# V in full-height blocks with half-zero copies, and a table and three splits moved to other places in VectorE's order

## The chip, the cores and the metric

The kernel runs on one core of one Trainium2 chip. The metric is device time in microseconds (us) of one launch. A core has a matmul engine (TensorE, PE), VectorE (DVE), ScalarE (ACT), GpSimd (POOL) and SyncE (SP), which work in parallel, each in the order of its own instructions, and wait for each other by semaphores. SBUF is the memory of 128 partitions that engines work on, PSUM the one that PE writes to. Transfers (DMAs) are issued from the queue of an engine, here mostly SP's; those that gather or scatter rows by index are built by GpSimd.

## The reference, cut to what matters

Three stages in a row: attention with a window, a gated dense layer, and a layer of eight experts in which a token goes to one expert or to none.

```python
# attention: 2 batches x 8 heads x 768 tokens x 64
scores = q @ k.T / 8 + bias(distance)       # only 8 global keys and the last 96 keys are kept
a = softmax(scores); attn = a @ v           # then heads side by side: x is 1536 x 512
# gated dense layer
xn = x / rms(x) * rms_g
x = (silu(xn @ w_gate) * (xn @ w_val)) @ w_out          # 512 -> 1536 -> 512
# experts
do_compute = x @ w_skip > 0
e = argmax(x @ w_gate2);  g = softmax(x @ w_gate2)[e]
out = x;  out[do] = x + g * (relu(x @ w1[e]) @ w2[e])   # 8 experts, 512 -> 1024 -> 512
```

## The kernel before, in words

**Attention.** Heads are taken in eight pairs, one head in each half of the partitions. A pair has three items, each of two blocks of 128 queries. Item by item PE makes scores (`qk`), DVE adds the bias and takes row maxima (`ttr`, L259), ACT takes exponentials (`exp`, L270), GpSimd or DVE scales (`norm`), PE transposes (`trans`) and multiplies with V (`pv`, L332). These steps run one loop turn apart: in turn t the loop makes the scores of item t and the product with V of item t − 3. A query block sees three blocks of keys, and of these one with half of its rows only. For such a half, V stands a second time in SBUF, the other half of the partitions cleared: tile `vlo` holds the rows of the even blocks on partitions 0 to 63, `vhi` those of the odd ones on 64 to 127. There are three pairs of such tiles, cleared once at the start by memsets on DVE and GpSimd, and reused by pair number modulo 3. `loadv` (L224) issues on SP the transfer of V itself (`vp`, 128 partitions) and of the two half tiles. Loads of a pair are issued two pairs ahead, in the order of a list on SP. The weights of the dense layer (`wraw`) come on the same queue, from the fourth pair of V on.

**Dense layer.** Products are made at full precision from parts: a weight is split in a high part (ACT casts) and a low part (DVE subtracts). The second product goes tile by tile, 12 tiles of 128 tokens. Into its order of matmuls the routing of each tile is hung by hooks: at given positions of the last tile, `routed(10)`, `tenth` (the ranks, selection and gates of tile 10) and `adds` are called. After the last tile comes the last routing: its logits, ranks, and the first rows of expert 0, one chain through PE, ACT and DVE. PE fills its waits there with products that nobody reads (`keep`).

**Experts.** Eight experts and one additional block of 64 tokens (`Job`, for an expert that has more than 128; it comes eighth in the row of nine, at index 7) run the same steps: `gather` (GpSimd fetches token rows by index), `tx` (transposition, high part `exh`, low part `exl`), `up` (first product), `relu`, `th` (transposition of the result into `ehh` and `ehl`), `down` (second product, into PSUM `epy`), `put` (gate, addition, scatter). A weight of 128 x 1024 comes as `eraw` and is split by ACT (`ewh`, L870) and DVE (`ewl`, L879). The order of these is fixed by the program: `split_next(n)` splits the next n chunks, in the row of all experts, `load_next(n)` issues the next n loads into free buffers. Buffers are a list of slots: those of the dense layer's output weights join it by `free_wo`. After expert 0's first product `jobs` makes a table of which expert needs additional blocks and how many (15 short DVE operations on counts that a small product gives), and `job_select` picks the block of the first. After the ninth `put` the number of blocks is read from the table as the bound of a loop, which here runs no further turn.

Of the kernel before, what the change touches and what calls it, by code (L numbers as in the profile page):

```python
# [127 lines left out]
def general_attention(s):  # L128

    nc, tc = s.nc, s.tc  # L130
    with tc.tile_pool(name="ga", bufs=1) as p, tc.tile_pool(name="gap", bufs=1, space=PSUM) as ps:
# [3 lines left out]
        with tc.For_i(0, 8, 1) as pr:  # L135
            slope = p.tile([128, 2], F32, name="gslope")
            nc.vector.tensor_copy(slope, slopes[:, ds(pr, 1), :].rearrange("p a b -> p (a b)"))
            for hh in range(2):
# [7 lines left out]
                v = p.tile([128, 11, 64], F32, name="gv")  # L146
                nc.sync.dma_start(v.rearrange("p (a b) d -> p a (b d)", a=1),
                                  s.vx.rearrange("a p n -> p a n")[:, ds(pr, 1), 704 * hh:704 * hh + 704])
                xo = p.tile([64, 768], F32, name="gxo")
# [52 lines left out]
def attention(s, rms):  # L202
# [21 lines left out]
    def loadv(pr):  # L224
        v = vs[pr] = ap.tile([128, 2, 11, 64], F32, name="vp", bufs=3)
        nc.sync.dma_start(v.rearrange("p h b d -> p (h b d)"), s.vx[pr, :, 0:1408])
        lo, hi = halves[pr % 3]
        nc.sync.dma_start(lo[0:64].rearrange("p h b d -> p (h b d)"), s.vx[pr, 0:64, 1408:2176])
        nc.sync.dma_start(hi[64:128].rearrange("p h b d -> p (h b d)"), s.vx[pr, 64:128, 1408:2048])

# [79 lines left out]
    def pv(it, r):  # L310
        pr, g = it
        pts = [(outs[it, z // 4][1], z % 4) for z in range(3 * r, 3 * r + 3)]

        if r == 0:
            po = s.bank([128, 512], "po")
            outs[it] = po[:, 0:256].rearrange("p (a b) -> p a b", a=2)
            s.spare = po[:, 256:512]
        po = outs[it]
        i = 2 * g + r
        lo, hi = halves[pr % 3]  # L320

        def terms(hh):
            a, b = slice(64 * hh, 64 * hh + 64), slice(64 - 64 * hh, 128 - 64 * hh)
            yield 0, 1, lo[:, hh, i], a
            if i:
                yield 0, 0, vs[pr][:, hh, 2 * i - 1], a
                yield 1, 1, hi[:, hh, i - 1], b
            yield 1, 2, vs[pr][:, hh, 2 * i], b

        for n, two in enumerate(zip(terms(0), terms(1))):  # L330
            for hh, (x, k, v, c) in enumerate(two):
                nc.tensor.matmul(po[64 * hh:64 * hh + 64, r, 64 * x:64 * x + 64], lhsT=v,  # L332
                                 rhs=pts[k][0][:, pts[k][1], c], start=i == 0 or n % 2 == 0, stop=i == 0 or n % 2 == 1)

    def out(it):
# [5 lines left out]
    n = len(items)  # L341
    halves = [(ap.tile([128, 2, 6, 64], F32, name=f"vlo{z}", bufs=1),
               ap.tile([128, 2, 5, 64], F32, name=f"vhi{z}", bufs=1)) for z in range(3)]
    es += [ap.tile([128, 2, 384], F32, name=f"es{z}", bufs=1) for z in range(3)]
    load(0)
    nc.gpsimd.memset(es[0][:, 0, 192:256], 0.0)
    for lo, hi in halves:
        nc.vector.memset(lo[64:128], 0.0)
        nc.gpsimd.memset(hi[0:64], 0.0)
    yield  # L350
# [392 lines left out]
def run(*parts):  # L743

    parts = list(parts)
    while parts:
        parts = [p for p in parts if next(p, FAR) is None]
# [13 lines left out]

def jobs(s, pool):

    nc, V = s.nc, s.nc.vector
    ps = s.ps_m.tile([128, 8], F32, name="cnt", tag="misc", bufs=1)
    nc.tensor.matmul(ps, lhsT=s.ones16, rhs=s.cum[:, 12, :], start=True, stop=True)
    s.i64 = pool.tile([128, 8, 22], F32, name="i64", bufs=1)
# [3 lines left out]
    nc.gpsimd.iota(s.i23, pattern=[[1, 23], [0, 8]], base=0, channel_multiplier=0,  # L771
                   allow_small_or_imprecise_dtypes=True)
    cnt = pool.tile([128, 8, 1], F32, name="cnts", bufs=1)
    V.tensor_copy(cnt.rearrange("p e a -> p (e a)"), ps)
# [70 lines left out]
class Expert:  # L845
# [37 lines left out]
    def split(self, c, hi, lo):  # L883
        self.high(c, hi)
        self.low(c, lo)
# [80 lines left out]
class Job(Expert):  # L966
# [54 lines left out]
    def down(self):  # L1021
        s = self.s
        self.y = s.ps_e.tile([128, 512], F32, name="epy", bufs=1)
        for k in range(8):
            self.products(self.y, self.hc[:, k], slice(512 * (k % 2), 512 * (k % 2) + 512),
                          *self.w[4 + k // 2][:2], k == 0, k == 7)
        for k in range(4, 8):
            self.done(k)
# [14 lines left out]
def attn_moe_kernel(ctx, tc, qx, kx, vx, rel, ints, wgv, w_out, rms_g, w9, w9t, w1, w2, out):  # L1043
# [317 lines left out]
    def tenth():  # L1361
        ranks(s, 10)
        choose(10, s.rk[10], s.oh[:, 10, 0:1])
        run(select(s, 10), gates(s, 10))

    def adds():
        add(s.x2[9], first[9], start=True)
        add(s.early, s.ident)
        free_wo(0, 3)

    def keep(n):
# [6 lines left out]
        (0, 2): lambda: turn(s, 10), (0, 5): early, (0, 9): lambda: routed(10),  # L1378
        (256, 4): lambda: turn(s, 11, 0), (256, 6): tenth, (256, 10): adds})
    idle = s.ps_m.tile([128, 512], F32, name="idle", tag="misc", bufs=1)  # L1380
    logits(s, 11, range(2))
# [29 lines left out]
    s.slots.add(s.epool, ["raw8"])  # L1411
    s.ps_e = pool(phase3, "ps_e", space=PSUM)
    experts[0].tx(x0)
    exps(s, 11)
    ranks(s, 11, s.ps_m, "misc")
    run(select(s, 11))

    def gathers():
        p = ids(s.ps_m, "misc", False)
        for t in range(9, 12):  # L1420
            nc.tensor.matmul(p, lhsT=s.sel[t][:, 0:128], rhs=s.val[:, t, 0, :], start=False, stop=t == 11)
        gi, si = indices(s, s.ixpool, p, 8, "s")
        for x in experts:
            if x is not job:
                x.gi, x.si = gi[:, x.e:x.e + 1], si[:, x.e:x.e + 1]
        for e in (1, 0, 2, 3):
            experts[e].gather()

        load_next(8, nc.gpsimd)

    experts[0].up(gathers)
    run(gates(s, 11))
    experts[0].relu()
    for t in range(9, 12):
# [15 lines left out]

    def split(n):
        split_next(n)
        load_next(max(0, len(s.slots.free) - 5))

    split(4)
    for j in range(9):
        if j:
            experts[j].th()
            split(1)
        if 1 <= j and j + 3 < 9:  # L1460
# [7 lines left out]
        if j == 0:  # L1468
            jobs(s, s.epool)
            job.gi, job.si, job.gate = job_select(s, s.epool, tabs[0:64, 1], slice(0, 1))  # L1470
        experts[j].down()
        split(3)
        experts[j].put()
    more = nc.values_load(s.eji[0:1, 23:24], min_val=1, max_val=22,  # L1474
                          skip_runtime_bounds_check_because="at most 22 blocks beyond the first ones")
    s.slots.free.sort(key=lambda x: x[1])
# [19 lines left out]
def layout(q, k, v):  # L1496
# [11 lines left out]
    for i in range(1, 6):  # L1508
        rows.append(np.concatenate([np.arange(128 * i - 96, 128 * i), np.arange(32)]))
        rows.append(np.arange(128 * i, 128 * i + 128))  # L1510
    vx = v[:, :, np.stack(rows, axis=1), :].reshape(B * H // 2, 2, 128, 11, D).transpose(0, 2, 1, 3, 4)
    half = np.zeros((B * H // 2, 128, 2, 6, D), v.dtype)
    half[:, 0:64] = vx[:, 0:64, :, 0::2]
    half[:, 64:128].reshape(B * H // 2, 64, 12 * D)[:, :, 0:10 * D] = \
        vx[:, 64:128, :, 1::2].reshape(B * H // 2, 64, 10 * D)
    return qx, kT[:, :, cols], np.concatenate([x.reshape(B * H // 2, 128, -1) for x in (vx, half)], axis=2)

# [50 lines left out]
```

## Time and profile before

| | |
|---|---|
| time, median of 3 runs | 533.31 us (532.67 to 535.36) |
| profiled execution | 531.11 us, span 529.4 us, mean clock of TensorE 0.995 |
| PE busy | 507.3 us, 96% of the span |
| DVE, ACT, GpSimd busy | 400.4, 265.5, 147.5 us |
| moved by DMA | 86.44 MB |

Attention runs to about 86 us, the dense layer and the routing of its tiles to about 397, the last routing to about 407, the experts to 522, and the last output and the end of the launch to 529.4. In a row of a timeline stand the start in us from the span's beginning, the duration, engine, line, operation, output <- inputs with their partitions x elements, the number of instructions that the row groups, and in brackets how long the engine was idle just before and what ended that. An idle engine costs time only if what waits for it reaches the end.

### The profile page before, as it was taken

The page shows a single profiled execution, that of the slowest core. Times are in us where ns is not written, and L with a number is a line of the kernel's source. Part 1 is how long each engine was busy: PE and PEld are TensorE (multiplying, and loading weights), DVE is VectorE, ACT ScalarE, POOL GpSimd, SP SyncE. Part 2 cuts the span into 40 slices and gives each one's busy share as a digit, 9 for nine tenths or more (in the row PEclk, how much of TensorE's full clock was granted, in tenths as well). Part 3 has the DMA queues.
Part 4 walks back from the last instruction along what each step waited for, and adds up shares of the span by engine and source line. Part 5 has one row for each costly group of instructions (what it writes and reads, how often), then busy time and mean ns, then how long its engine had stood idle before and what let it go on. Part 6 is the DMA issues. An engine that isn't in the chain of part 4 may idle for free. (4 is left out here: it accounts for less than half of the span.)

```text
span 529.4 us, 9730 instructions
## 1 busy us (share of the span) xinstructions
PE 507.3 (96%) x3389; PEld 413.6 (78%) x3389; DVE 400.4 (76%) x988; ACT 265.5 (50%) x618; POOL 147.5 (28%) x201
## 2 busy tenths in 40 slices
PE   7798999999999999999999999999999999999994
PEld 6676778888888888778888887877898778888763
DVE  7789896588887788588854467767743699999981
ACT  3898993333232332323323525425521779888860
POOL 4666772112222222212211000000000703666101
PEclk9999999999999999999999999999999999999997
DMA  5997811322332323323217213313771899999300
GB/s 183 303 310 228 271 34 43 139 80 85 116 111 82 125 87 113 119 80 119 81 42 252 86 41 119 120 40 127 239 279 41 307 399 396 399 400 384 120 16 16
DMA packets 31391, 86.44 MB, mean 163 GB/s; under 512 B 3875, under 2 KB 4271, under 8 KB 31336
## 3 DMA queue, kind: packets, MB, share of 16 engines
q1 hardware_dynamic: 26856, 74.52, 41.0%
q0 software_dynamic: 2608, 8.09, 4.0%
q10 hardware_dynamic: 1872, 3.15, 1.7%
q8 instruction: 28, 0.46, 0.4%
q14 instruction: 27, 0.22, 0.1%
HBM read 78.05 MB, written 8.53 MB: 164 GB/s over the span
## 5 line engine op out<-in xcount | busy, mean ns | idle before, releaser
L547 PE MATMUL ps<-xh,wh 128*128 128x512 f32 x272 | 106.3, 391 | 1.4 <-DVE h L567 1.4
L547 PE MATMUL ps<-xl,wh 128*128 128x512 f32 x272 | 106.1, 390 | 0.0
L547 PE MATMUL ps<-xh,wl 128*128 128x512 f32 x272 | 106.0, 390 | 0.0
L879 DVE TENSOR_TENSOR ewl<-eraw,ewh 128x1024 fp32r<-128x1024 f32 x72 | 83.4, 1215 | 7.7 <-ACT ewh L870 7.6
L870 ACT CAST ewh<-eraw 128x1024 fp32r<-128x1024 f32 x72 | 71.3, 1054 | 7.0 <-DVE ewl L879 6.8
L498 DVE SCALAR_TENSOR_TENSOR wraw<-f64t,wraw 128x512 f32<-128x512 f32 x36 | 43.7, 1214 | 29.6 <-ACT f64t L496 29.6
L625 PE MATMUL px<-woh,hh 128*128 128x512 f32 (+1 forms) x156 | 61.3, 393 | 0.0
L547 PEld LDWEIGHTS ps<-xh,wh 128*128 128x128 f32 x272 | 51.1, 188 | 12.2 <-DVE h L567 1.8
L547 PEld LDWEIGHTS ps<-xh,wl 128*128 128x128 f32 x272 | 51.1, 188 | 10.4
L547 PEld LDWEIGHTS ps<-xl,wh 128*128 128x128 f32 x272 | 51.1, 188 | 10.3
L625 PE MATMUL px<-woh,hl 128*128 128x512 f32 (+1 forms) x156 | 58.5, 375 | 0.0
L625 PE MATMUL px<-wol,hh 128*128 128x512 f32 (+1 forms) x156 | 58.3, 374 | 0.0
L511 POOL TENSOR_TENSOR wl<-f64t,wh 128x512 fp32r<-128x512 f32 x23 | 29.7, 1293 | 98.4 <-ACT wh L510 60.7
L510 ACT CAST wh<-f64t 128x512 fp32r<-128x512 f32 x24 | 14.9, 622 | 79.8 <-DVE f64t L508 79.8
L270 ACT ACTIVATE es<-es,m 128x192 f32<-128x192 f32 (+1 forms) x96 | 41.2, 432 | 6.4 <-DVE m L259 6.4
L287 POOL TENSOR_SCALAR es<-es,z 128x192 f32<-128x192 f32 (+1 forms) x94 | 36.9, 412 | 24.7 <-DVE z L279 10.7
L579 DVE TENSOR_TENSOR hl<-h,hh 128x256 fp32r<-128x256 f32 x72 | 25.4, 422 | 17.9 <-ACT hh L578 17.8
L625 PEld LDWEIGHTS px<-woh,hl 128*128 128x128 f32 x156 | 29.3, 188 | 5.6
L625 PEld LDWEIGHTS px<-woh,hh 128*128 128x128 f32 x156 | 29.4, 188 | 5.5 <-issue 0.8
L625 PEld LDWEIGHTS px<-wol,hh 128*128 128x128 f32 x156 | 29.4, 189 | 4.2
L1357 POOL DMA_INDIRECT early<-xm,si_f x1 | 1.3, 1301 | 106.8 <-DMA out_dram<-x 106.8
L259 DVE CUSTOM_DVE_ANT_0 es<-sc,bias 128x192 f32<-128x192 f32 (+1 forms) x96 | 27.0, 337 | 5.4 <-PE sc L248 3.6
(240 smaller groups left out, 1035.4 us busy)
## 6 DMA issues: line engine op xcount, KB each, us to landing
eraw<-in_w_dram SPq DMA_DIRECT2D x64, 512.0 KB, 11.6
wraw<-in_wgv_dram SPq DMA_DIRECT2D x24, 512.0 KB, 3.9
wraw<-in_w_out_dram SPq DMA_DIRECT2D x12, 512.0 KB, 3.4
vp<-in_vx_dram SPq DMA_DIRECT2D x8, 704.0 KB, 7.8
eraw<-in_w_dram POOLq DMA_DIRECT2D x8, 512.0 KB, 14.5
kd<-in_kx_dram SPq DMA_DIRECT2D x7, 464.0 KB, 8.7
xm<-x SPq DMA_DIRECT2D x12, 256.0 KB, 2.6
out_dram<-x ACTq DMA_DIRECT2D x12, 256.0 KB, 2.9
```

The source lines that it names most:

```text
L259: nc.vector.tensor_tensor_reduce(out=e[:, r, e0:e0 + n], in0=sc[x][:, r, 0:n], in1=s.bias[:, pr % 4, b0:b0 + n], scale=-0.125, scalar=3.0e ...
L270: nc.scalar.activation(e[:, r, e0:e0 + n], e[:, r, e0:e0 + n], AF.Exp, bias=m[:, j:j + 1], scale=-1.0, accum_out=z[:, j:j + 1])
L287: eng.tensor_scalar(e[:, r, e0:e0 + n], e[:, r, e0:e0 + n], z[:, j:j + 1], one[0], ALU.mult, *one[1:])
L498: nc.vector.scalar_tensor_tensor(out=a.bitcast(F32), in0=t, scalar=F64_LEAST, in1=a.bitcast(F32), op0=ALU.is_ge, op1=ALU.mult)
L510: nc.scalar.copy(hi, t)
L511: eng.tensor_tensor(lo, t, f(hi), ALU.subtract)
L547: nc.tensor.matmul(p, lhsT=w[:, k, :], rhs=x[c][:, k, a:b], start=n == 0, stop=n == 11)
L579: nc.vector.tensor_tensor(hl[:, i, :], src, f(hh[:, i, :]), ALU.subtract)
L625: nc.tensor.matmul(p, lhsT=h[:, k, :], rhs=w[k][:, c:c + N], start=n == 0, stop=n == 35)
L870: eng.copy(wh, raw)
L879: eng.tensor_tensor(wl, raw, f(wh), ALU.subtract)
L1357: nc.gpsimd.indirect_dma_start(out=s.early, out_offset=None, in_=s.xm[0:1152, :], in_offset=bass.IndirectOffsetOnAxis(ap=si, axis=0), boun ...
```

## The change

Three things change.

1. V. The host lays V out as 11 blocks of (plain, half-zero copy) x (head 0, head 1) x 64. One tile `vp` of 128 partitions holds all of it; the zeros come with the transfer. `loadv` makes three transfers, of blocks 0 to 2, 3 to 6 and 7 to 10. The two kinds of half tile and their memsets go. The products take the same numbers from the new places.
2. The table of additional blocks. Its constants are made before the gathers, its count product is issued with the gathers' hook inside expert 0's first product, and its DVE operations come right after the gates of the last tile. `job_select` stays.
3. Splits and loads. `free_wo(0, 3)` and `split_next(3)` move into `tenth`, so that three splits come before the last routing's steps. `load_next(3)` comes after the last tile; the hook of the gathers loads 6 chunks in place of 8; further loads follow the table. The gathers go in the order of experts 1, 2, 0, 3.

Beside these, the additional block's second product gets a PSUM bank of its own (`jy`), its `put` comes after the last expert's `th`, and the loop bound is read before the last `put`.

```diff
     def loadv(pr):
-        v = vs[pr] = ap.tile([128, 2, 11, 64], F32, name="vp", bufs=3)
-        nc.sync.dma_start(v.rearrange("p h b d -> p (h b d)"), s.vx[pr, :, 0:1408])
-        lo, hi = halves[pr % 3]
-        nc.sync.dma_start(lo[0:64].rearrange("p h b d -> p (h b d)"), s.vx[pr, 0:64, 1408:2176])
-        nc.sync.dma_start(hi[64:128].rearrange("p h b d -> p (h b d)"), s.vx[pr, 64:128, 1408:2048])
+        v = vs[pr] = ap.tile([128, 11, 2, 2, 64], F32, name="vp", bufs=3)
+        for a, b in ((0, 3), (3, 7), (7, 11)):
+            nc.sync.dma_start(v[:, a:b].rearrange("p b z h d -> p (b z h d)"), s.vx[pr, :, 256 * a:256 * b])
...
-            yield 0, 1, lo[:, hh, i], a
+            yield 0, 1, v[:, 2 * i, 1, hh], a
             if i:
-                yield 0, 0, vs[pr][:, hh, 2 * i - 1], a
-                yield 1, 1, hi[:, hh, i - 1], b
-            yield 1, 2, vs[pr][:, hh, 2 * i], b
+                yield 0, 0, v[:, 2 * i - 1, 0, hh], a
+                yield 1, 1, v[:, 2 * i - 1, 1, hh], b
+            yield 1, 2, v[:, 2 * i, 0, hh], b
...
-    for lo, hi in halves:
-        nc.vector.memset(lo[64:128], 0.0)
-        nc.gpsimd.memset(hi[0:64], 0.0)
...
-    ps = s.ps_m.tile([128, 8], F32, name="cnt", tag="misc", bufs=1)
-    nc.tensor.matmul(ps, lhsT=s.ones16, rhs=s.cum[:, 12, :], start=True, stop=True)
...
     def down(self):
         s = self.s
-        self.y = s.ps_e.tile([128, 512], F32, name="epy", bufs=1)
+        self.y = s.ps_x.tile([128, 512], F32, name="jy", tag="x0", bufs=1)
...
         run(select(s, 10), gates(s, 10))
+        free_wo(0, 3)
+        split_next(3)
 
     def adds():
         add(s.x2[9], first[9], start=True)
         add(s.early, s.ident)
-        free_wo(0, 3)
...
         (256, 4): lambda: turn(s, 11, 0), (256, 6): tenth, (256, 10): adds})
+    load_next(3)
...
+    job_consts(s, s.epool)
     experts[0].tx(x0)
...
+    cnt = s.ps_x.tile([128, 8], F32, name="cnt", tag="x0", bufs=1)
+
     def gathers():
+        nc.tensor.matmul(cnt, lhsT=s.ones16, rhs=s.cum[:, 12, :], start=True, stop=True)
...
-        for e in (1, 0, 2, 3):
+        for e in (1, 2, 0, 3):
             experts[e].gather()
 
-        load_next(8, nc.gpsimd)
+        load_next(6, nc.gpsimd)
...
     experts[0].up(gathers)
     run(gates(s, 11))
+    jobs(s, s.epool, cnt)
+    load_next(max(0, len(s.slots.free) - 5))
     experts[0].relu()
...
             experts[j].th()
+            if j == 8:
+                job.put()
             split(1)
...
         if j == 0:
-            jobs(s, s.epool)
             job.gi, job.si, job.gate = job_select(s, s.epool, tabs[0:64, 1], slice(0, 1))
         experts[j].down()
         split(3)
-        experts[j].put()
-    more = nc.values_load(s.eji[0:1, 23:24], min_val=1, max_val=22, ...
+        if j == 8:
+            more = nc.values_load(s.eji[0:1, 23:24], min_val=1, max_val=22, ...
+        if j != 7:
+            experts[j].put()
...
-    return qx, kT[:, :, cols], np.concatenate([x.reshape(B * H // 2, 128, -1) for x in (vx, half)], axis=2)
+    half = vx.copy()
+    half[:, 64:128, 0::2] = 0
+    half[:, 0:64, 1::2] = 0
+    return qx, kT[:, :, cols], np.stack([vx, half], axis=3).reshape(B * H // 2, 128, -1)
```

SP's queue at the start of attention, before, from q and k of the second pair on (`vlo` and `vhi` with a number are the half tiles of one pair):

```order
L217 DMA qd<-in_qx_dram 128x768
L218 DMA kd<-in_kx_dram 128x928
L226 DMA vp<-in_vx_dram 128x1408
L228 DMA vlo_95<-in_vx_dram 64x768
L229 DMA vhi_96<-in_vx_dram 64x640
L226 DMA vp<-in_vx_dram 128x1408
L228 DMA vlo_97<-in_vx_dram 64x768
L229 DMA vhi_98<-in_vx_dram 64x640
L217 DMA qd<-in_qx_dram 128x768
```

and after:

```order
L217 DMA qd<-in_qx_dram 128x768
L218 DMA kd<-in_kx_dram 128x928
L227 DMA vp<-in_vx_dram 128x768
L227 DMA vp<-in_vx_dram 128x1024 x2
L227 DMA vp<-in_vx_dram 128x768
L227 DMA vp<-in_vx_dram 128x1024 x2
L217 DMA qd<-in_qx_dram 128x768
```

The order of pairs is the same; a pair's V comes in three transfers over all partitions.

DVE around the last routing and expert 0, before, from the last gates (`val`, L712) to the table (`cnts`, `jw`); `slt` numbers the tokens' places, `exl`, `ehl` and `ewl` are low parts:

```order
L712 TENSOR_TENSOR val<-rg,val 128x8
L1437 TENSOR_TENSOR slt_5024<-slt,sl 24x256
L941 TENSOR_TENSOR ehl<-eht,ehh 128x512 x2
L910 TENSOR_TENSOR exl<-ext,exh 128x512
L1444 COPY tabs<-tab 128x48
L1446 TENSOR_TENSOR gate<-tabs 128x8
L879 TENSOR_TENSOR ewl<-eraw,ewh 128x1024 x8
L910 TENSOR_TENSOR exl<-ext,exh 128x512
L774 COPY cnts<-cnt 128x8
L776 TENSOR_TENSOR jw<-cnts,i_5146 128x176
```

and after, from the gates of tile 10 on (first three rows) and, behind the rows left out, from the last gates on:

```order
L705 TENSOR_TENSOR val<-rg,val 128x8
L875 TENSOR_TENSOR ewl<-eraw,ewh 128x1024 x3
L665 TENSOR_REDUCE rm<-lg 128x1
...
L705 TENSOR_TENSOR val<-rg,val 128x8
L770 COPY cnts<-cnt 128x8
L772 TENSOR_TENSOR jw<-cnts,i_4931 128x176
...
L793 TENSOR_SCALAR eji<-jpre 128x1
L1445 TENSOR_TENSOR slt_5063<-slt,sl 24x256
L937 TENSOR_TENSOR ehl<-eht,ehh 128x512 x2
```

Three splits now stand ahead of the last tile's first routing step `rm`, and the table ahead of `slt`.

DVE at the last expert, before: the additional block's output (L1034, L1035) ahead of the last expert's `ehl`.

```order
L1018 SCALAR_TENSOR_TENSOR ehh<-exl,ehh 128x4x64
L879 TENSOR_TENSOR ewl<-eraw,ewh 128x1024 x5
L1034 TENSOR_TENSOR eo<-epy,eo 64x512
L1035 SCALAR_TENSOR_TENSOR eo<-eo,jb,exg 64x512
L941 TENSOR_TENSOR ehl<-eht,ehh 128x512 x2
L959 SCALAR_TENSOR_TENSOR eo<-epy,gate,exg 128x512
```

and after:

```order
L1014 SCALAR_TENSOR_TENSOR ehh<-exl,ehh 128x4x64
L875 TENSOR_TENSOR ewl<-eraw,ewh 128x1024 x2
L937 TENSOR_TENSOR ehl<-eht,ehh 128x512 x2
L1030 TENSOR_TENSOR eo<-jy,eo 64x512
L1031 SCALAR_TENSOR_TENSOR eo<-eo,jb,exg 64x512
L1479 TENSOR_LOAD eji
L955 SCALAR_TENSOR_TENSOR eo<-epy,gate,exg 128x512
```

The block's output stands behind `ehl`, and three splits fewer are left at this place.

## Rows read from the trace of the kernel before

**Rows 1.** The page's first part, busy us of each engine

```profile
PE 507.3 (96%) x3389; PEld 413.6 (78%) x3389; DVE 400.4 (76%) x988; ACT 265.5 (50%) x618; POOL 147.5 (28%) x201
```

**Rows 2.** By stage: us, busy PE PEld DVE ACT POOL, clock, DMA share, GB/s

```profile
30.00:86.00 56.00, 52.59 (x948) 40.73 (x946) 50.24 (x215) 48.58 (x194) 38.55 (x84) 1.00 0.59 179
407.00:522.00 115.00, 111.68 (x533) 88.56 (x531) 102.15 (x139) 85.29 (x113) 44.34 (x27) 1.00 0.74 279
```

**Rows 3.** Timeline at the first product with V

```profile
17.30 0.34 PE L332 MATMUL po<-pts,vlo 128*64 128x64 f32 x4 [0.74 <-DMA vlo<-in_vx_dram]
19.61 0.46 ACT L270 ACTIVATE es<-es,m 128x192 f32<-128x192 f32 x1 [0.60 <-DVE m L259]
```

**Rows 4.** DMA issues of attention: KB each, median us from issue to landing

```profile
vp<-in_vx_dram SPq DMA_DIRECT2D x8, 704.0 KB, 7.8
vlo<-in_vx_dram SPq DMA_DIRECT2D x8, 192.0 KB, 7.5
```

**Rows 5.** Four stretches with full queues, columns as in rows 2

```profile
12.00:14.00 2.00, 2.00 (x33) 1.64 (x27) 1.86 (x11) 1.30 (x7) 0.68 (x2) 1.00 0.97 393
14.40:20.40 6.00, 4.58 (x76) 3.71 (x78) 4.62 (x25) 4.65 (x20) 3.63 (x10) 1.00 1.04 267
24.00:30.00 6.00, 5.45 (x111) 4.33 (x110) 4.35 (x23) 5.02 (x22) 3.17 (x9) 1.00 1.03 310
440.00:470.00 30.00, 30.00 (x148) 24.63 (x147) 30.00 (x31) 25.78 (x34) 14.37 (x4) 1.00 1.04 400
```

**Rows 6.** Timeline, ACT's first step on a weight chunk

```profile
36.95 0.67 ACT L496 ACTIVATE f64t<-wraw 128x512 f32<-128x512 f32 x1
```

**Rows 7.** Timeline at the start, behind the memsets

```profile
3.83 0.16 DVE L67 SCALAR_TENSOR_TENSOR intt<-ints 128x2 f32<-128x2 int32 x1 [0.50 <-DMA ints<-in_ints_dram]
```

**Rows 8.** The page's costliest groups, the two halves of a weight split

```profile
L879 DVE TENSOR_TENSOR ewl<-eraw,ewh 128x1024 fp32r<-128x1024 f32 x72 | 83.4, 1215 | 7.7 <-ACT ewh L870 7.6
L870 ACT CAST ewh<-eraw 128x1024 fp32r<-128x1024 f32 x72 | 71.3, 1054 | 7.0 <-DVE ewl L879 6.8
```

**Rows 9.** Timeline, last routing, ACT and DVE

```profile
401.33 0.47 ACT L629 ACTIVATE x<-px,r 128x256 f32<-128x256 f32 x1 [4.07 <-PE px L625]
403.41 0.17 DVE L672 TENSOR_REDUCE rm<-lg 128x1 f32<-128x8 f32 x1 [4.18 <-PE lg L600]
```

**Rows 10.** DVE's stretch of the table, then timeline around it

```profile
427.45:431.19 3.74, 3.27 (x16) 1.00 1.05 410
436.46 0.48 PE L951 MATMUL epy<-ewh,ehh 128*128 128x512 f32 x1 [0.76 <-DVE eo L959]
414.02 0.41 DVE L1437 TENSOR_TENSOR slt<-slt,sl 24x256 f32<-24x256 f32 x1 [3.28 <-PE sl L739]
```

**Rows 11.** Timeline, gathers on GpSimd, and PE behind the first

```profile
410.32 1.01 POOL L894 DMA_INDIRECT exg<-xm,gi_s  x1 [16.08 <-DVE rz L705]
437.98 1.61 POOL L894 DMA_INDIRECT exg<-xm,gi_s  x1 [0.31 <-issue]
415.50 0.66 PE L905 MATMUL ext<-ident,exg 128*128 128x128 f32 x4 [0.27 <-DMA exg<-xm,gi_s]
```

**Rows 12.** Timeline, transpositions, ehl and products of an early and the last expert

```profile
414.08 1.14 PE L938 MATMUL eht<-ident,eh 128*128 128x128 f32 x8
415.46 1.29 DVE L941 TENSOR_TENSOR ehl<-eht,ehh 128x512 fp32r<-128x512 f32 x2 [1.03 <-ACT ehh L940]
513.13 1.03 PE L938 MATMUL eht<-ident,eh 128*128 128x128 f32 x8
514.94 0.47 PE L951 MATMUL epy<-ewh,ehh 128*128 128x512 f32 x1 [0.77 <-DVE eo L1034]
516.23 0.50 PE L951 MATMUL epy<-ewh,ehl 128*128 128x512 f32 x1 [0.58 <-DVE ehl L941]
```

**Rows 13.** Timeline in attention, a wait of PE and of ACT

```profile
24.55 0.28 PE L332 MATMUL po<-pts,vhi 128*64 128x64 f32 x3 [1.28 <-issue]
25.04 0.47 ACT L429 ACTIVATE xh<-po,rg 128x256 fp32r<-128x256 f32 x1 [0.62 <-PE po L332]
```

More of the change, by code (lines that the diff above doesn't have):

```diff
@@ L146, in general_attention @@
                 v = p.tile([128, 11, 64], F32, name="gv")
-                nc.sync.dma_start(v.rearrange("p (a b) d -> p a (b d)", a=1),
-                                  s.vx.rearrange("a p n -> p a n")[:, ds(pr, 1), 704 * hh:704 * hh + 704])
+                nc.sync.dma_start(v.rearrange("p (a b) d -> p a b d", a=1),
+                                  s.vx.rearrange("a p (b z d) -> p a b z d", z=4, d=64)[:, ds(pr, 1), :, hh])
                 xo = p.tile([64, 768], F32, name="gxo")
@@ L319, in pv @@
         i = 2 * g + r
-        lo, hi = halves[pr % 3]
+        v = vs[pr]
         def terms(hh):
             a, b = slice(64 * hh, 64 * hh + 64), slice(64 - 64 * hh, 128 - 64 * hh)
-            yield 0, 1, lo[:, hh, i], a
+            yield 0, 1, v[:, 2 * i, 1, hh], a
             if i:
-                yield 0, 0, vs[pr][:, hh, 2 * i - 1], a
-                yield 1, 1, hi[:, hh, i - 1], b
-            yield 1, 2, vs[pr][:, hh, 2 * i], b
+                yield 0, 0, v[:, 2 * i - 1, 0, hh], a
+                yield 1, 1, v[:, 2 * i - 1, 1, hh], b
+            yield 1, 2, v[:, 2 * i, 0, hh], b
         for n, two in enumerate(zip(terms(0), terms(1))):
-            for hh, (x, k, v, c) in enumerate(two):
-                nc.tensor.matmul(po[64 * hh:64 * hh + 64, r, 64 * x:64 * x + 64], lhsT=v,
+            for hh, (x, k, w, c) in enumerate(two):
+                nc.tensor.matmul(po[64 * hh:64 * hh + 64, r, 64 * x:64 * x + 64], lhsT=w,
                                  rhs=pts[k][0][:, pts[k][1], c], start=i == 0 or n % 2 == 0, stop=i == 0 or n % 2 == 1)
@@ L341, in attention @@
     n = len(items)
-    halves = [(ap.tile([128, 2, 6, 64], F32, name=f"vlo{z}", bufs=1),
-               ap.tile([128, 2, 5, 64], F32, name=f"vhi{z}", bufs=1)) for z in range(3)]
     es += [ap.tile([128, 2, 384], F32, name=f"es{z}", bufs=1) for z in range(3)]
@@ L759, in indices, with job_consts @@
     return gi, si
-def jobs(s, pool):
-    nc, V = s.nc, s.nc.vector
-    ps = s.ps_m.tile([128, 8], F32, name="cnt", tag="misc", bufs=1)
-    nc.tensor.matmul(ps, lhsT=s.ones16, rhs=s.cum[:, 12, :], start=True, stop=True)
+def job_consts(s, pool):
+    nc = s.nc
     s.i64 = pool.tile([128, 8, 22], F32, name="i64", bufs=1)
@@ L772, in jobs @@
                    allow_small_or_imprecise_dtypes=True)
+def jobs(s, pool, ps):
+    V = s.nc.vector
     cnt = pool.tile([128, 8, 1], F32, name="cnts", bufs=1)
@@ L1425, in gathers, with split @@
                 x.gi, x.si = gi[:, x.e:x.e + 1], si[:, x.e:x.e + 1]
-        for e in (1, 0, 2, 3):
+        for e in (1, 2, 0, 3):
             experts[e].gather()
-        load_next(8, nc.gpsimd)
+        load_next(6, nc.gpsimd)
+    def split(n):
+        split_next(n)
+        load_next(max(0, len(s.slots.free) - 5))
     experts[0].up(gathers)
     run(gates(s, 11))
+    jobs(s, s.epool, cnt)
+    load_next(max(0, len(s.slots.free) - 5))
     experts[0].relu()
@@ L1449, in attn_moe_kernel @@
             x.gate = gate[:, x.e:x.e + 1]
-    def split(n):
-        split_next(n)
-        load_next(max(0, len(s.slots.free) - 5))
     split(4)
@@ L1472, in attn_moe_kernel @@
         split(3)
-        experts[j].put()
-    more = nc.values_load(s.eji[0:1, 23:24], min_val=1, max_val=22,
-                          skip_runtime_bounds_check_because="at most 22 blocks beyond the first ones")
+        if j == 8:
+            more = nc.values_load(s.eji[0:1, 23:24], min_val=1, max_val=22,
+                                  skip_runtime_bounds_check_because="at most 22 blocks beyond the first ones")
+        if j != 7:
+            experts[j].put()
     s.slots.free.sort(key=lambda x: x[1])
@@ L1510, in layout @@
         rows.append(np.arange(128 * i, 128 * i + 128))
[L1511 to L1515, printed above, removed]
-    return qx, kT[:, :, cols], np.concatenate([x.reshape(B * H // 2, 128, -1) for x in (vx, half)], axis=2)
+    vx = v[:, :, np.stack(rows, axis=1), :].reshape(B * H // 2, 2, 128, 11, D).transpose(0, 2, 3, 1, 4)
+    half = vx.copy()
+    half[:, 64:128, 0::2] = 0
+    half[:, 0:64, 1::2] = 0
+    return qx, kT[:, :, cols], np.stack([vx, half], axis=3).reshape(B * H // 2, 128, -1)
 def relative():
```

## The prediction, made before the changed kernel was run

> **What bounds the kernel now.** I read the page's busy times first: TensorE (PE) works 507.3 of 529.4 us of span at full clock, the next engine, VectorE (DVE), 400.4 [rows 1]. The change takes no matmul away and makes none shorter, so it can win only where PE stands still or another engine paces a stage. Second, the table by stage [rows 2]: in attention (30 to 86 us) PE, DVE and ScalarE (ACT) work 52.59, 50.24 and 48.58 of 56.00 us, so that a tile's way through all three paces it as much as any one; the experts, 407 to 522, leave PE 3.32 us idle. Third, I read timelines only where PE stands still next to something that the diff touches: the first products with V, the first output of an expert, and the last expert.
>
> **The change, part by part.** Sums are made on the profiled execution, 531.11 us with a span of 529.4; the median of the three runs shown is 533.31, so I subtract the sum from that.
>
> *V's first load.* The first product with V starts at 17.30 after 0.74 us of waiting for vlo, the second of three transfers of its pair [rows 3]. In its wake ACT, which takes the exponentials behind PE's scores and DVE's row maxima, is idle 0.60 us at 19.61 until such a maximum is there. With the new order the first product needs only blocks 0 to 2, the first 384 KB of the pair, so this wait goes. What has reached ACT at the end of that way is what the stage feels: −0.6 us (ends 0 and −0.74).
>
> *V's extra bytes.* A pair had 704 + 192 KB [rows 4] and 160 more for vhi (64 x 640 words), 1056 KB in all, and has 384 + 512 + 512 = 1408 KB. Are they free? Where only transfers over 128 partitions run (12.00 to 14.00, 440 to 470) the queues move 393 to 400 GB/s; where vlo and vhi are under way they move 267 (14.40 to 20.40) and 310 (24 to 30), with the queues' engines about as full, 0.97 to 1.04 [rows 5]. So a half-partition transfer takes engine time without bytes. If vlo and vhi go at half the 393, a pair takes 704 KB / 393 + 352 KB / 196 = 1.83 + 1.84 = 3.67 us; the new pair takes 1408 KB / 393 = 3.67 us. Equal: 0.
> The Trainium skill's page "SBUF — State Buffer", section "Door 1: The DMA port swizzle (why `[64,N]` ≈ `[32,N]`)", says that partitions 0 to 63 reach only half of the memory's ports, and 64 to 127 the other half. By that rule the sum is the same 0; the drop to 267 GB/s agrees with it.
> The sum has two ends. The nearest later consumer is the weight chunk wraw, queued behind V of pair 3 and read by ACT at 36.95 with no idle time [rows 6]. From about 12 us, where the first of these transfers begin to land, to there V of four pairs, q and k of pairs 2 and 3 (128 x 768 and 128 x 928 words each) and 512 KB of wraw must land: 5632 + 1696 + 512 = 7840 KB = 8.03 MB, which needs 8.03 / 24.95 = 322 GB/s. At 393 wraw lands at 32.4, no cost; were the low rate of 267 kept in spite of the new layout, it would land at 42.1, 5.1 us late. I take 0, by the rows at 393 and 400 for transfers of this shape.
>
> *Cleared halves.* Three memsets on DVE and three on GpSimd vanish at the start. DVE's next operation waits 0.50 us for the integers' transfer at 3.83 anyway [rows 7], and what follows hangs on it: 0.
>
> *Three splits moved before the last routing.* They cost DVE 3 × 1.215 = 3.65 us and ACT 3 × 1.054 = 3.16 [rows 8]. DVE is next needed at 403.41, after 4.18 us of idle time: 4.18 − 3.65 = 0.53 to spare. ACT is next needed at 401.33, after 4.07: 0.91 to spare [rows 9]. Cover: the wait for the last tile's logits. Without that cover the routing would start late and PE with it, since everything from 403.41 on is one chain: at most one piece, +1.2. I take 0. The buffers that the moved splits free are loaded earlier on SP's queue, and from then on every split stands three chunks ahead in program order, so that the loads run nearer to the splits; 440 to 470 shows these loads at 400 GB/s: 0, and rival E if that is too little.
>
> *Table of additional blocks moved.* Its fifteen short operations hold DVE's queue from 427.45 to 431.19, 3.74 us, 3.27 of them busy [rows 10]. Behind them are three more splits, and behind those the first expert's output eo, which PE needs to be out of its PSUM bank: 0.76 us of waiting at 436.46. With the table gone, everything behind it and eo with them comes 3.74 us earlier, against 0.76 that are needed: −0.76, which is the one end too; the other is 0, if the splits now wait for weights. At its new place the table fills a DVE wait of 3.28 us before 414.02 (for PE's sl) and ends near 410.74 + 3.74 = 414.48, so slt comes 0.46 later. Queued behind it on DVE is ehl, which has its own wait of 1.03 us for ACT before 415.46 [rows 12], and PE transposes slt only after the next tile's transpositions at 415.50 [rows 11]: 0. The count product goes to PE earlier, one small matmul either way; its PSUM tile is read in the table's first operation, before the next tenant at 415.50.
>
> *Gathers beside the table.* Four gathers are built on GpSimd from 410.32 to 415.25, now beside the table's operations. With DVE on short operations one takes 1.01 us; beside splits on DVE one took 1.61 [rows 11]. If the first is drawn out so, the transposition of its tile, at 415.50 after 0.27 us of wait, comes 0.6 later; against that SP's weight loads, which were issued into the same queue time at 410.86, are now in part earlier, which may take away the 0.27. Value 0, ends −0.27 and +0.6.
> The Trainium skill speaks against the change here: "SBUF — State Buffer", section "SBUF: two separate sides", says that some DVE operations lock a port which GpSimd needs to write descriptors, and GpSimd then waits whole instructions out. The 1.61 beside 1.01 agrees; by it the sum would be +0.6 for this part.
>
> *The last expert.* PE turns from the additional block to the last expert's transpositions at 513.13 and stands still for 0.77 us before 514.94, because ACT copies that block's result out of PSUM ahead of casting ehh, and DVE adds its halves and the gate ahead of ehl; another 0.58 us go at 516.23 for ehl [rows 12]. Now the block has its own bank and its output comes behind: At an earlier expert ehl began 1.38 us after the first transposition (414.08 to 415.46, its two halves in 1.29) with nothing in between; here that gives 513.13 + 1.38 = 514.51, the first half of ehl done at 515.16, and the third product, which waits for it, at about 515.23 in place of 516.23: −1.00 (ends −0.58, the wait at 516.23 alone, and −1.35, both waits). The block's output then lies beside the last expert's products, and so does the loading of the loop count, now ahead of the last output, for which DVE only waits.
>
> Sum: −0.60 − 0.76 − 1.00 = −2.36 us: profiled 531.11 to 528.75, median 533.31 to **530.9 us**.
>
> **The rivals.**
> B. The first stage keeps its pace: the 0.60 us are lost again at the next slow step, for example at 24.55, where PE stood still for 1.28 us for nothing that the profile names [rows 13]. For it: no engine is full from 30 to 86, so there is slack in which a late step is made up. Against: three are over 86% busy there, and the slack of each is a wait for another. Then −1.76: 531.5.
> C. Slower: V's larger pairs keep the queues at 267 GB/s although the halves are gone, since each block now brings a third more bytes; wraw lands 5.1 us late, ACT waits for it in its order with the exponentials behind it, and all of attention shifts. It decides below 322 GB/s. For it: 24 to 30 has 310. Against: vlo and vhi are in flight there. +5.1 − 1.76 = +3.3: 536.6.
> D. More comes back: the wait at 24.55 stands before a product with vhi, and ACT pays 0.62 us behind it at 25.04 [rows 13]; if a half transfer is its cause, these go too: −2.98, 530.3. Against: the profile names no transfer there.
> E. It does not do what it says: the moved splits or the gathers eat the gains of the experts' stage. The splits, three chunks ahead, find their weights not landed, so that the −0.76 is lost and the routing starts one piece late (+1.2): −0.4, 532.9. It decides where a load lands later than its three chunks of lead.
>
> **How the numbers follow.** Forecast .50, B .16, C .09, D .14, E .11. The forecast's own range, its small terms at either end, is 529.9 to 532.1. For 8 in 10 I take in D whole, B, and most of E, and leave most of C out, with the spread of the runs shown (532.67 to 535.36) on the upper side: 528.3 to 533.9. A measurement can tell about 0.5%, 2.67 us, from no change; 530.64 is the border for faster. D, two fifths of the forecast, and a little of B are below it: .14 + .21 + .05 = .40. Slower than 535.98 are C and a remnant: .10. The rest, .50, is the same.
>
> **What would show it.** In the new profile: no wait for a V transfer at the first product near 17.3, and at least 380 GB/s from 14 to 20 us; ACT's read of wraw near 36.3 with no idle time; DVE's rm at the last routing still waiting for PE, with three splits in front; the table's fifteen operations before slt, and no PE wait for eo at 436; gathers still near 1.0 us; at the last expert one PE wait below 0.5 in place of 0.77 and 0.58. It is wrong if DMA waits show up before 90 us, or if PE's idle time in 407 to 522 stays above 2.5 us.

## The result, and the profile after

The changed kernel takes 527.5 us (median of 6 runs, 526.73 to 528.60) where the kernel before takes 533.46 (6 runs, 532.35 to 535.36): ratio 0.9904, 95% interval 0.9883 to 0.9924, so 4.1 to 6.2 us faster, 5.1 by the ratio. Forecast were 2.4 us and 530.9, with 528.3 as lower end: the sign was right, the size too small, and the time lies below the range. The profiled execution took 528.0 us with a span of 526.3, only 3.1 below that of before, which was one of the fastest of its kernel. So two questions stood: which part gave more than forecast, and what the profile of before had not shown.

The page, first part, and the stretches that answer to [rows 1, 2 and 5]; columns as there:

```profile
PE 507.0 (96%) x3389; PEld 414.0 (79%) x3389; DVE 398.5 (76%) x985; ACT 265.4 (50%) x618; POOL 144.5 (27%) x196
```

```profile
30.00:86.00 56.00, 53.10 (x939) 41.28 (x938) 50.40 (x214) 48.70 (x191) 38.62 (x83) 1.00 0.59 214
407.00:522.00 115.00, 109.39 (x523) 87.23 (x522) 98.38 (x131) 81.95 (x108) 43.18 (x24) 1.00 0.74 269
...
14.40:20.40 6.00, 5.58 (x105) 4.28 (x100) 5.17 (x26) 5.21 (x24) 3.62 (x10) 1.00 1.02 405
24.00:30.00 6.00, 6.00 (x117) 4.66 (x118) 4.82 (x25) 5.30 (x23) 3.78 (x9) 1.00 1.03 404
```

PE's work is the same; the queues now move 404 to 405 GB/s where it was 267 and 310. The window of the experts ends 3 us after PE's last product here; up to that product, 407 to 518.9, PE is idle for 2.5 us, where it was 3.0 before.

Timeline of the changed kernel at the places of [rows 3, 6, 9, 11, 12 and 13], then a row of the kernel before that I had not read:

```profile
16.75 0.92 PE L330 MATMUL po<-pts,vp 128*64 128x64 f32 x24
24.00 0.77 PE L246 MATMUL sc<-kd,qd 64*64 64x64 f32 x16 [1.04 <-DMA kd<-in_kx_dram]
35.01 0.68 ACT L489 ACTIVATE f64t<-wraw 128x512 f32<-128x512 f32 x1
...
401.52 0.17 DVE L665 TENSOR_REDUCE rm<-lg 128x1 f32<-128x8 f32 x1 [0.77 <-PE lg L593]
408.42 1.04 POOL L890 DMA_INDIRECT exg<-xm,gi_s  x1 [15.18 <-DVE rz L698]
415.00 0.66 PE L901 MATMUL ext<-ident,exg 128*128 128x128 f32 x4 [1.65 <-DMA exg<-xm,gi_s]
435.20 1.62 POOL L890 DMA_INDIRECT exg<-xm,gi_s  x1 [0.31 <-issue]
512.70 0.51 PE L947 MATMUL epy<-ewh,ehh 128*128 128x512 f32 x1 [0.24 <-ACT ehh L936]
513.42 0.50 PE L947 MATMUL epy<-ewh,ehl 128*128 128x512 f32 x1
```

```profile
32.22 0.66 PE L297 MATMUL pt<-ident,es 128*128 128x128 f32 x4 [1.09 <-POOL es L287]
```

The wait for V at the first product is gone. So are the 1.28 us before the product at 24.55 (a wait for kd, the keys, of 1.04 stands behind it instead) and the wait of 1.09 us of a transposition at 32.22. The wait for kd is a DMA wait ahead of 90 us, which the prediction had named as a sign of being wrong. From one such place to the next the same matmul is early by 0.56, 2.01, 0.94 (behind kd) and 2.19 us, and at 68 us by 1.97. At the first gathered tile PE waits 1.65 us in place of 0.27: there 1.4 us are given back. Behind it the first output (no wait) and the last expert (0.24 in place of 0.77 and 0.58) bring the lead to 2.8 at the last product; the launch ends 3.1 us earlier.

### The profile page after: what moved, and what is told of

Read it like the earlier page. It is cut to its first block, busy times and chain, and to the rows that moved or that the text cites. A ratio compares the mean times of both kernels' runs of the same rounds, so it can differ in the third digit from the quotient of the medians.

```text
span 526.3 us, 9732 instructions
## 1 busy us (share of the span) xinstructions
PE 507.0 (96%) x3389; PEld 414.0 (79%) x3389; DVE 398.5 (76%) x985; ACT 265.4 (50%) x618; POOL 144.5 (27%) x196
## 4 chain that ended last, share of the span: by engine, by line
PE 51%; DVE 12%; issue 9%; DMA 4%; ACT 4%; another core or an unknown queue 0%; POOLq 0%; ACTq 0%; POOL 0%; DVEq 0%
PE px L618 17%; PE ps L540 11%; PE eph L915 8%; PE epy L947 7%; DVE f64t L498 3%; DVE f64t L501 3%; ACT f64t L489 3%; DVE f64t L496 2%; DMA wraw<-in_wgv_dram 1%; DMA wraw<-in_w_out_dram 1%; DMA exg<-xm,gi_s 1%; PE lg L593 1%; PE eht L934 1%; DVE w9b L601 1%; DVE h L560 1%
## 5 line engine op out<-in xcount | busy, mean ns | idle before, releaser
L491 DVE SCALAR_TENSOR_TENSOR wraw<-f64t,wraw 128x512 f32<-128x512 f32 x36 | 43.8, 1216 | 29.5 <-ACT f64t L489 29.5
```

The source lines that it names most:

```text
L491: nc.vector.scalar_tensor_tensor(out=a.bitcast(F32), in0=t, scalar=F64_LEAST, in1=a.bitcast(F32), op0=ALU.is_ge, op1=ALU.mult)
```

## The experiments

Kernels that are parts of the change are named by the parts they hold; "before" in a ratio is always a run of the kernel before on the same chip.

**V alone.** The kernel before with `loadv`, `pv`, the memsets and the host's layout as after.

> The kernel before with V's new layout and three transfers alone. Theory F (full height): a transfer into 64 partitions holds the queues at about 267 GB/s, and the whole of attention comes about 2.0 us earlier without it, as the two profiles show at 68 us; the rest of the measured 5 to 6 us, which the profiled execution of before did not have to give, is V's too, because half-height transfers cost a varying time. Then 3.5 to 4.5 us faster than before, and 400 GB/s from 14 to 20 us. Rival M: the rest comes from the experts' stage. Then 2.0 us faster, not more.

529.79 us (12 runs, 529.34 to 530.84), ratio 0.9938 (0.9916 to 0.9961): 3.3 us faster, 2.1 to 4.5 by the interval. That is a little under theory F's 3.5 to 4.5, and rival M's 2.0 lies just outside the interval. The rate from 14 to 20 us is 388 GB/s where 400 was expected:

```profile
14.40:20.40 6.00, 5.44 (x100) 4.31 (x100) 5.31 (x26) 5.23 (x24) 3.61 (x10) 1.00 1.00 388
24.00:30.00 6.00, 6.00 (x118) 4.66 (x111) 5.07 (x25) 5.44 (x24) 3.78 (x10) 1.00 1.03 406
```

No execution showed a granted clock below 0.994, where 7 of 29 of the kernel before showed 0.987 to 0.991, at 533.6 to 536.1 us.

**All but V.**

> The kernel before with everything but V's part: table, splits, loads, gathers, and the last expert's order. Theory F: 1.1 us faster, the first output and the last expert giving 0.75 + 1.2 and the later gather taking back 1.4 to 1.7 less 0.5. Rival M: 3 us or more faster.

532.44 us (12 runs, 530.19 to 535.05), ratio 0.9988 (0.9963 to 1.0012): between nothing and 2 us. Rival M is out. Six of the 12 executions have a mean clock of 0.986 to 0.992. Its profiled execution took 534.18 us and shows two falls of the clock, each behind a wait of PE. The waits, then the windows around them:

```profile
25.20 0.28 PE L332 MATMUL po<-pts,vhi 128*64 128x64 f32 x3 [1.82 <-issue]
418.43 1.01 PE L908 MATMUL ext<-ident,exg 128*128 128x128 f32 x4 [1.52 <-DMA exg<-xm,gi_s]
```

```profile
24.00:26.00 2.00, 0.81 (x22) 0.73 (x23) 0.42 (x3) 0.84 (x4) 1.12 (x3) 1.00 1.04 263
26.00:28.00 2.00, 2.00 (x18) 1.24 (x10) 1.34 (x9) 1.50 (x7) 0.50 (x2) 0.52 1.03 239
...
418.00:420.00 2.00, 1.34 (x6) 0.89 (x6) 0.42 (x1) 0.52 (x2) 2.00 (x4) 0.65 0.82 240
420.00:424.00 4.00, 3.88 (x9) 3.11 (x10) 3.87 (x6) 3.47 (x5) 0.79 (x2) 0.50 0.96 360
```

Behind both PE works at 1.2 GHz, by the trace's clock records for 3.4 us (26.1 to 29.5) and 6.8 us (418.6 to 425.4). The second fall is dear: against the profile of before the same matmul is 2.9 us late at the end of the wait and 5.6 at 428 us. The first is made up in part: 0.6 late behind the wait, 2.1 at 29, 0.9 at 33, where the kernel before has a wait of its own, and 1.3 from 60 us to the end of attention.

**V in half-height transfers, and V in one transfer.** On V alone:

```diff
-            nc.sync.dma_start(v[:, a:b]..., s.vx[pr, :, 256 * a:256 * b])
+            for p in (slice(0, 64), slice(64, 128)):
+                nc.sync.dma_start(v[p, a:b]..., s.vx[pr, p, 256 * a:256 * b])
```

```diff
-        for a, b in ((0, 3), (3, 7), (7, 11)):
+        for a, b in ((0, 11),):
```

> As v_only, but each of V's three transfers is issued as two, one for partitions 0 to 63 and one for 64 to 127: the same bytes, the same tile, the same products. Theory F (the height of a transfer sets its rate): the queues fall to 200 to 270 GB/s from 14 to 30 us, products or scores wait for transfers, and the time is 2 to 6 us above v_only. Rival N (what mattered was the first third and fewer small tiles): the rate stays near 400 and the time is that of v_only within 0.7 us.

> As v_only, but V of a pair comes in one transfer of 1408 KB over 128 partitions in place of three. Theory F: same as v_only within 0.7 us, since 1408 KB at 393 GB/s take 3.7 us and land before 17 us. Rival T (the first third is what ends the wait at the first product with V): the first product waits 0.5 us or more for vp, and 0.5 to 1 us of the gain are gone.

Half height: 543.65 us, ratio 1.0204 (1.0165 to 1.0243), 10.9 us slower than before, 14 above V alone, with the same bytes. Windows and the worst wait:

```profile
14.40:20.40 6.00, 5.65 (x106) 4.32 (x100) 5.30 (x26) 5.22 (x23) 3.60 (x10) 1.00 1.04 255
24.00:30.00 6.00, 0.89 (x16) 0.75 (x16) 0.00 (x0) 0.71 (x2) 1.62 (x4) 0.77 1.03 270
```

```profile
29.11 1.34 PE L247 MATMUL sc<-kd,qd 64*64 64x64 f32 x16 [5.19 <-DMA kd<-in_kx_dram]
```

The height of a transfer sets its rate, 255 to 270 GB/s against 388 and 406 in V alone, with the DMA share at 1.00 to 1.04 in all four stretches. The number of transfers does not: the kernel with one moves 410 and 417 GB/s in the same stretches. This is also what rival C of the prediction would have looked like. The Trainium skill, "SBUF — State Buffer", section "“Can I just issue two DMAs to hit both halves?”", says that two transfers into the two halves of the partitions do not add up; the 255 agrees.

One transfer: 530.25 us, ratio 0.9947 (0.9923 to 0.9971), the same as V alone within noise, although the first product waits just as before, since the transfer did not land before 17 us as expected:

```profile
17.30 0.92 PE L330 MATMUL po<-pts,vp 128*64 128x64 f32 x24 [0.73 <-DMA vp<-in_vx_dram]
```

So the wait on which my 0.6 us rested is worth little at the end; what counts is the rate behind it.

**The changed kernel again, with loads behind the gathers, without the moved splits and loads, and with k ahead of V.** The edits of the second and the fourth:

```diff
     jobs(s, s.epool, cnt)
-    load_next(max(0, len(s.slots.free) - 5))
+    load_next(max(0, len(s.slots.free) - 5), nc.gpsimd)
```

```diff
     loadv(0)
-    loadv(1)
...
                 load(pr + 2)
+                if pr == 0:
+                    loadv(1)
```

> The changed kernel itself, on the chip of the three that follow, as their reference. Expected 527.5 us, and a granted clock of 0.994 or more in each execution, where the kernel before shows 0.987 to 0.991 in about a quarter of its own.

> The changed kernel, but the loads that follow the table are issued on GpSimd's queue, behind the gathers, in place of SP's. Theory Q (the four loads that SP issues from 402 to 409 us stand in the queues ahead of the first gather's rows): the first gather lands about 1.5 us sooner, PE's wait of 1.65 us at 415 goes to 0.3 or less, and the time falls by 1.3 us. Rival P (the gather is slow because GpSimd builds it beside the table): PE's wait stays above 1.2 us and the time is the same.

> V's part, the table and the last expert's order, without the moved splits and loads and with the gathers' old order. Theory Q: no wait of more than 0.4 us at the first gather, 0.5 to 1.5 us faster than the changed kernel. Rival S (the moved splits give the rest of the gain): 0.5 us or more slower than the changed kernel, and a wait for eo or for weights comes back in the experts' stage.

> The changed kernel, but SP issues q and k of the third pair ahead of V of the second. Theory K (what is left at 24 us is the queue in front of k): PE's wait of 1.04 us for kd at 24.00 goes, and the time falls by 0.7 to 1.0 us. Rival A (ACT and DVE pace that stretch anyway): the wait goes or moves, and the time is the same within 0.4 us.

| kernel, all on one chip | median us (range) | ratio to before (95%) |
|---|---|---|
| changed kernel | 528.10 (527.48 to 530.16) | 0.9917 (0.9888 to 0.9946) |
| loads behind the gathers | 528.30 (526.94 to 528.67) | 0.9909 (0.9879 to 0.9938) |
| without moved splits and loads | 527.09 (526.79 to 527.74) | 0.9891 (0.9862 to 0.9920) |
| k ahead of V | 528.53 (526.81 to 529.12) | 0.9908 (0.9877 to 0.9939) |

PE's row at the first gathered tile in the first three, and behind it the clock of the changed kernel's second profile:

```profile
414.93 0.66 PE L901 MATMUL ext<-ident,exg 128*128 128x128 f32 x4 [1.26 <-DMA exg<-xm,gi_s]
```

```profile
414.68 0.60 PE L901 MATMUL ext<-ident,exg 128*128 128x128 f32 x4
```

```profile
413.92 0.66 PE L901 MATMUL ext<-ident,exg 128*128 128x128 f32 x4 [0.18 <-DMA exg<-xm,gi_s]
```

```profile
416.00:418.00 2.00, 1.74 (x5) 1.39 (x6) 1.72 (x4) 2.00 (x3) 1.53 (x3) 0.64 0.85 262
```

The loads are the cause of the gather's wait (theory Q's mechanism; rival P is out, the gathers take 0.99 to 1.04 us beside the table in all three), and the clock can fall behind this wait too: two of the changed kernel's seven executions had 0.992, where 0.994 or more was expected of each. What the wait costs in time is less clear. The third kernel is 1.0 us faster than the changed one, but it also has the gathers in their old order; the second, which differs in the loads alone, lost its wait and not its time. In its profile PE's unread products between 8 and 11 us ran at half rate and attention began 1.8 us late, as in 4 of 16 profiles, of four kernels; but that is one execution of six, and a profile of the third kernel had it too. The same profile ends 8.5 us behind the start of its last product, the changed kernel's 7.8; why was not looked for. So the order of the gathers stays as a rival for the 1.0 us. With k ahead of V the wait at 24.00 went and one of 1.27 us came at 38.65: rival A.

**Which of the rest gives what.** The kernel without moved splits and loads again, as reference; the same with only the splits moved (`free_wo(0, 3)` and `split_next(3)` in `tenth`); V and the last expert's order, with the table at its old place. The fourth kernel is V alone without the unread products:

```diff
-        if t < 4:
-            product(s, unread, (7, 4, 3, 2)[t])
```

> V's part, the table and the last expert's order without the moved splits and loads, as before (v_tt), as reference for the three that follow: 527.1 us, 0.5 to 1.0 below the changed kernel, and no execution with a granted clock below 0.994.

> As v_tt, with the three splits moved ahead of the last routing, but the loads and the order of the gathers as in the kernel before. Theory Q (the loads cost, the splits hide in the wait for the logits): same as v_tt within 0.5 us, no wait above 0.4 us at the first gather. Rival E (the splits themselves make the last routing late): 0.7 us or more above v_tt, and DVE's rm starts without idle time.

> V's part and the last expert's order alone, the table at its old place. By the profiles: PE's wait for eo at 435 is back with 0.76 to 0.88 us, so 0.8 us above v_tt, and 1.2 us below V's part alone (529.8). Rival: the table at its new place delays slt and the gathers by as much as it gives, and the time is that of v_tt.

> V's part alone, without the products that nobody reads in the first four turns of attention (16 products of 128 columns fewer, nothing else). Theory C (what PE does in its waits there holds the granted clock): the clock falls to 1.2 GHz for some us between 10 and 30 us in many executions, the mean is below 0.992, and the time is 1 to 4 us above V's part alone (529.8), although PE has less to do. Rival D (only the transfers matter): the time is that of V's part alone within 0.5 us, the clock 0.994 or more.

526.82 us (525.91 to 528.03); 526.70 (526.12 to 527.87); 528.71 (12 runs, 527.60 to 530.76); 529.27 (12 runs, 528.53 to 529.89). So the splits cost and give nothing. DVE still waits for PE behind them (first row, from the second kernel); with the table at its old place PE waits for eo again (second row, from the third):

```profile
402.86 0.17 DVE L665 TENSOR_REDUCE rm<-lg 128x1 f32<-128x8 f32 x1 [0.77 <-PE lg L593]
```

```profile
434.65 0.47 PE L944 MATMUL epy<-ewh,ehh 128*128 128x512 f32 x1 [0.89 <-DVE eo L952]
```

The table's new place gives 1.9 us by these medians; the wait for eo that it removes is 0.89, so about 1 us of it is not accounted for by a row. The last expert's order gives 1.0 by the ratios to the kernel before, 0.9919 (0.9892 to 0.9945) against 0.9938 of V alone; these are from two chips and their intervals overlap, so the 1.0 is not shown by times alone. The fourth kernel surprised both theories: the clock fell, as theory C had it, and the time did not rise, as rival D had it.

```profile
10.00:12.00 2.00, 0.99 (x3) 0.42 (x3) 1.97 (x12) 1.46 (x7) 1.56 (x4) 0.96 0.74 229
12.00:14.00 2.00, 0.69 (x2) 0.29 (x2) 1.94 (x12) 1.30 (x7) 1.08 (x4) 0.50 0.95 303
14.00:16.00 2.00, 1.95 (x19) 1.44 (x20) 1.97 (x10) 1.38 (x7) 0.81 (x3) 0.50 0.92 300
```

All 12 executions had a mean clock of 0.990 to 0.994, and the ratio is 0.9925 (0.9900 to 0.9950), against 0.9938 of V alone on another chip. Against V alone's profile the same exponential is 1.0 us late at 20 us and 0.6 at 61; the end of attention is not late, but V alone lost 0.7 of its own between. It also has 16 products less to do, so the price of the fall alone is not measured. With the 1.3 us that stay in all-but-V's profile, a fall early in attention costs little; one behind the gather cost 2.7 us there, and 1.5 in the changed kernel's second profile, where it lasted 3.4 us. That PE's slack to the other engines makes the difference is argued.

**V as before under the better experts' part, and the kernel before again.**

> The table and the last expert's order with V as before: v_tt without V's part. Theory F: 3.3 us above v_tt (about 530.2), of which 2 are PE's waits near 17, 24 and 32 us and the rest comes in executions in which these waits are longer or the clock falls behind them. Rival M (V and the experts' part work only together): 1.5 us or less above v_tt, or no gain over the kernel before.

> The kernel before once more, for a second profile. Theory F: PE's waits of 0.7 to 1.8 us near 17, 24 and 32 us are there again, with lengths that differ by 0.5 us or more from the first profile, and if the mean clock is below 0.992 the stretch at 1.2 GHz lies behind one of them, before 35 us. Rival M: attention ends within 0.3 us of the first profile, and what differs lies behind 400 us.

> A third profile of the kernel before, with the same expectations as the second.

The first: 529.47 us (7 runs, 527.89 to 531.60), ratio 0.9942 (0.9916 to 0.9968). Against 0.9878 and 0.9891 with the new V that is 2.7 to 3.4 us for V on this base too. The two further profiles of the kernel before are single executions, of 530.90 and 529.88 us. PE's waits of attention in them, one fence each:

```profile
17.70 0.34 PE L332 MATMUL po<-pts,vlo 128*64 128x64 f32 x4 [1.09 <-DMA vlo<-in_vx_dram]
24.94 0.28 PE L332 MATMUL po<-pts,vhi 128*64 128x64 f32 x3 [1.27 <-issue]
```

```profile
23.08 0.28 PE L332 MATMUL po<-pts,vhi 128*64 128x64 f32 x3 [0.53 <-issue]
23.95 0.77 PE L248 MATMUL sc<-kd,qd 64*64 64x64 f32 x16 [0.41 <-DMA kd<-in_kx_dram]
30.84 0.65 PE L297 MATMUL pt<-ident,es 128*128 128x128 f32 x4 [0.70 <-POOL es L287]
```

The wait near 24 us is there each time, with 0.53 to 1.82 us over five profiles with the old V; the others are not: the third profile has none at 17, the second only 0.27 near 32. The third ends attention 1.1 us ahead of the first, the variation that theory F expected; the second ends it 0.2 ahead, within rival M's 0.3. Neither caught a fall of the clock.

What ends the wait near 24 us, for which the rows say "issue", can be read from the kept traces. They hold the transfers of instructions beside those of data. On one of the two instruction queues (q8) a transfer of 16 KB landed at 23.07, 23.28, 21.63, 23.57 and 24.12 us in the five profiles with the old V, and PE went on 1.45 to 1.66 us later each time. The same holds for every wait of PE from 18 us to the end of attention that has "issue" and 0.3 us or more, in all profiles: 14 waits, 1.36 to 1.66 us behind such a landing. In the changed kernel and in V alone that transfer landed at 20.48 and 20.37, and PE did not wait. When it started, PE had begun 217 to 228 matmuls in the five profiles, 221 with V in half height, and 173 to 205 in the ten with V over all partitions and all unread products. So PE waited for its instructions, which came later in its work with half-height transfers in the queues. That q8 carries PE's instructions is inferred from these distances; no run moved that transfer alone.

## Why the prediction was wrong

The step that failed is *V's first load*: −0.6 us, with ends 0 and −0.74, where V's part measured −3.3 (2.1 to 4.5). The mechanism was named in the next paragraph, a half-height transfer takes the queues' time without bytes, but I priced it only at the one wait whose releaser is a transfer of V and used it otherwise to show that the extra bytes are free. That was right (ACT reads wraw at 35.01 with no idle time), and too little. The queues at 267 to 310 GB/s delayed what came through them: V itself at 17 us, PE's instructions at 24, by the traces, and after these the third wait, at 32. For that one the row names GpSimd; it ends 1.38 us behind a landing on q8 like the others, but that the queues are its cause is not shown. Rival D named the second, with 0.62 us and .14; nothing named the third. Nor was wraw the nearest later consumer: the keys are, at 24 us, with 1.04 us of wait in the changed kernel and 5.19 with V in half height. The vanished memsets gave nothing: at 10 us the same matmul starts within 0.02 us of before.

Between the profiles the lead is 1.9 us at the last routing, and 1.3 in V alone's profile, of which 1.0 is left at the end. The rest of the 3.3 lies between executions. On V alone's chip the 22 executions of the kernel before with a mean clock of 0.994 or more average 532.3 us, the 7 others 535.3, V alone 529.9: 2.4 us against the former, and 0.7 more because of the latter. The profile of before, at 531.11, was faster than either average, and I subtracted from the median a sum read in it.

*Three splits moved*: right, cost 0; DVE had 0.77 us to spare where 0.53 were forecast. *Loads and gathers*: wrong in sign. I had expected that the earlier loads would leave the queues to the first gather; the four that follow the table in program order, which SP issues as soon as a buffer is free, stood in them instead. Value 0 with an end of +0.6; measured +1.65 − 0.27 = 1.4 us of PE's time and, if the order of the gathers is free, about 1.0 of the kernel's. The gathers themselves are not drawn out beside the table (0.99 to 1.04 us); the port that the Trainium skill warns of in "SBUF — State Buffer", section "SBUF: two separate sides", shows in no row there, and 1.62 beside the splits stayed as it was. That row was the mild end: four later gathers took 6.1 to 6.2 us in both profiles, without a wait of PE for them. *Table*: mechanism right, wait gone, −0.76 forecast, −1.1 between the profiles (expert 0's second product, 422 to 447 us), −1.9 by medians. *The last expert*: −1.00 forecast, −1.1 between the profiles, −1.0 by ratios of two chips. Summed by parts: −3.3 − 1.0 − 1.9 + 1.0 = −5.2, against −5.1 measured. That the parts add up is not shown so closely: without V the last three gave −0.6 in place of −1.9, while the table and the last expert alone gave −3.1 on the old V. There the moved loads, with the order of the gathers, cost some 2.5 us by the ratios, and in the profile the clock fell behind the gather's wait.

The best version found is the change without the moved splits and loads: 527.09 and 526.82 us, the first 1.0 below the changed kernel on the same chip and 1.1 to 1.2% below the kernel before.

## What to carry to other kernels

When a kind of transfer is found to waste the queues' time, its price is the sum over everything that waits behind it in the stage, instructions too, so list every wait of the stage before and after pricing one. Issue bulk loads behind a small transfer that an engine is about to wait for: here that took the wait away, though with the loads alone moved no time was gained. And subtract a sum only from the time of the execution in which it was read: where runs spread by 1%, one profile shows one draw.

## What the runs showed that I had not expected

A PE wait of 1.2 to 1.8 us was followed by a fall of the clock in some executions (1.20, 1.26, 1.52, 1.82 us) and not in others (1.27, 1.28, 1.31, 1.65). And at the start the unread products ran at half rate in 4 of 16 profiles; here two executions of one kernel, the fourteen products of turn 0 and 1 in each:

```profile
7.78 1.83 PE L86 MATMUL unread<-ones 128*128 128x128 f32 x14
```

```profile
8.29 3.15 PE L86 MATMUL unread<-ones 128*128 128x128 f32 x14
```

The windows give 1.00 as the clock there, but the trace's clock records say more: the first record of the upper level, 2.4 GHz, starts at 5.97 us in the first of these executions and at 11.08 in the second, at 10.6 to 11.4 in the four profiles and at 4.7 to 7.0 in all others. Ahead of it the unread products follow each other in 0.21 us, behind it in 0.11 from the second of a row on. So it was the clock that rose later; why it did in these four is open.
